# 480 bytes left unused above the right-hand tiles of SBUF

## The chip, the cores and the metric

The kernel runs on one core of one Trainium2 chip. The metric is the device time of one execution in microseconds (us), the median of several runs; lower is better.

## What is computed

All arrays are float32.

```python
def phi(x):                                   # q, k: (4, 8, 576, 64)
    proj = einsum('bhsd,df->bhsf', x, w_phi)  # 128 features
    proj = proj - max(abs(proj), axis=-1)
    return concatenate([exp(proj), exp(-proj)], axis=-1)
...
num = einsum('bhsf,bhfd->bhsd', q_p, einsum('bhsf,bhsd->bhfd', k_p, v))
den = einsum('bhsf,bhf->bhs', q_p, sum(k_p, axis=2)) + 1e-06
x = (num / den) as 2304 tokens x 512
...
h = x @ w_in                                  # 512 x 2048
x = (h * sigmoid(1.702 * h)) @ w_out          # 2048 x 512
...
p = domain_probs / (domain_probs.sum(-1) + 1e-09)
for e in range(4):
    out += p[:, e:e + 1] * (maximum(x @ w1[e], 0.0) @ w2[e])   # 512 x 1024, 1024 x 512
```

## The kernel before

The first stage is the attention: 16 pairs of heads, whose steps stand in one long written list (`ORDER`) that fixes the order on every engine. Its tiles lie in the pool `ap`. Two expert layers follow: layer 1 (sigmoid) and layer 2 (four experts with relu). They are cut into 48 units. Units 0 to 7 are layer 1 on the tokens 0 to 1279 (group 0), 8 to 15 layer 1 on the other 1024 tokens (group 1), 16 to 31 layer 2 on group 0, 32 to 47 layer 2 on group 1. A unit covers 256 hidden columns.

In a unit u the first products (x @ w_in) of u alternate with the second products (hidden @ w_out) of the unit before it, u - 1:

- Units 0 to 7 (`plain_unit`) make their first products directly: line 718 multiplies 128x512 tiles, line 741 the rest of group 0 in 128x256 tiles.
- All other units (`strassen_unit`) make seven products of six matmuls each (line 660); units of group 0 add the rest at line 741.
- The second products are line 776 in layer 1 and line 778 in layer 2. Their tile of hidden values is called `g`, or `gr` for the rest.

Each product of two float32 tiles is made of three matmuls of type fp32r: high part by high part, high by low, low by high (`PASSES`). A matmul has a stationary operand, which a weight load (PEld in the profile) puts into the array, and a moving operand, which streams through it in 512 columns (2048 bytes of each partition) or 256 columns. TensorE's order is the order of the code. Work that prepares the next units (`background`: casts and subtractions of weights on ScalarE and GpSimd, tiles of x on VectorE) is strung between the steps and pinned to them on each engine.

Two pools hold the operands, and they grow towards each other:

- `ep`, on the left (line 112), holds `xo0` to `xo6` (x, built by `build_x`), the raw weights, and `win` of the even units. The program's own allocation puts its first tile at byte 38,400 of a partition, a multiple of 512, and all of its sizes are multiples of 2048 bytes, so each of its tiles begins at a multiple of 512.
- `lp`, on the right (line 615, opened where `ap` was closed), holds `win` of the odd units (line 209: `pools[u % 2]`), `wout` of all units (line 233), `g` and `gr` (line 626), the rest `xr` of x (line 288), and the scratch tiles `sg`, `m1`, `uu` and `h`. It hangs from the right end of the usable bytes, 229,344, which is 32 more than a multiple of 64, and 480 more than a multiple of 512. All of its tiles have sizes that are multiples of 2048 bytes, so each begins 32 bytes past a multiple of 64.

The offsets of the operands inside their tiles are multiples of 512 bytes. So before the change the operands are placed like this, where "0" means at a multiple of 64 bytes and "32" means 32 bytes past one:

| line | product | stationary | moving |
|---|---|---|---|
| 718, 660, even unit | first | `win` in `ep`: 0 | `xo` in `ep`: 0 |
| 718, 660, odd unit | first | `win` in `lp`: 32 | `xo` in `ep`: 0 |
| 741, even unit | first, rest | `win` in `ep`: 0 | `xr` in `lp`: 32 |
| 741, odd unit | first, rest | `win` in `lp`: 32 | `xr` in `lp`: 32 |
| 776 | second, layer 1 | `wout` in `lp`: 32 | `g`, `gr` in `lp`: 32 |
| 778 | second, layer 2 | `g`, `gr` in `lp`: 32 | `wout` in `lp`: 32 |

The tiles of the attention's pool `ap` hang from the same end; most begin 32 bytes past a multiple of 64, a few small ones at one (of the two buffers of `kv`, one each).

Of the kernel before, what the change touches and what calls it, by code (L numbers as in the profile page):

```python
# [9 lines left out]
F32 = mybir.dt.float32  # L10
# [8 lines left out]
P = 128  # L19
# [21 lines left out]
D1 = D + 1  # L41
NB32 = 2 * S // 32
WARM = 7
ES_DVE = "0000000000000001"
FH_DVE = "0101010111011100"
BUFS = {
# [57 lines left out]
def fused(ctx: ExitStack, tc: tile.TileContext, qT, kT, v, w_phi, wg1, wg2, probs, out):  # L104
# [5 lines left out]
    dram = ctx.enter_context(tc.tile_pool(name="dram", bufs=1, space=bass.MemoryType.DRAM))  # L110

    ep = ctx.enter_context(tc.tile_pool(name="ep", bufs=1, reuse_waits="tile"))
    ap_cm = tc.tile_pool(name="ap", bufs=1, side="right", reuse_waits="tile")
    ap = ap_cm.__enter__()

# [13 lines left out]
    def warm(n):  # L129
        for _ in range(n):  # L130
            nc.tensor.matmul(ps_n[:, 0:HALF], zero[:, 0, 0, 0:P], zero[:, 0, 0, :], start=True, stop=True)

    warm(WARM)

# [212 lines left out]
    class Pair:  # L347
# [79 lines left out]
        def es(self):  # L427
            t = self.eq[:, 0, :]
            eng = nc.vector if ES_DVE[self.i] == "1" else nc.gpsimd
            eng.tensor_tensor(out=t, in0=t, in1=self.mb, op=ALU.subtract)  # L430
# [512 lines left out]
```

## Time and profile before

| | |
|---|---|
| median of 3 runs | 1320.72 us (1319.97 to 1321.62) |
| span of the profiled execution | 1319.6 us; its own time isn't listed apart from the three runs |
| attention | 0 to 161 us of the span |
| layer 1, units 0 to 15 | 161 to 549 us |
| layer 2, units 16 to 47 | 549 to 1316 us |
| TensorE busy | 1296.2 us (98%) |
| VectorE, ScalarE, GpSimd busy | 758.1 (57%), 524.6 (40%), 659.9 us (50%) |

A matmul's record runs until its last column has left the array, and the next matmul begins long before that. So the pace of TensorE isn't read from the length of a record but from the starts: the start of one group of matmuls taken from the start of the next one, divided by the number of matmuls in between. The timeline merges neighbouring matmuls of the same line and the same tiles into one row and gives its start to 0.01 us.

### The profile page before, as it was taken

What the parts mean: (1) busy time and instruction counts of PE and PEld (TensorE: products, weight loads), DVE (VectorE), ACT (ScalarE), POOL (GpSimd) and SP (SyncE); (2) the same over time, 40 slices, a digit from 0 to 9 for tenths busy, and PEclk for the clock granted to TensorE, in tenths of its full rate; (3) what the DMA queues carried; (4) which work ended last, traced back from release to release, by engine and by line L of the source; (5) the groups of instructions that cost most, each with busy time, mean ns of one, the idle gap of its engine ahead of it and who ended that gap; (6) DMA issues with size and microseconds to landing.
All of it is one profiled execution on the core that took longest, in us unless ns stands there. A gap on an engine that the chain in (4) does not pass through costs nothing.

```text
span 1319.6 us, 19956 instructions
## 1 busy us (share of the span) xinstructions
PE 1296.2 (98%) x8241; PEld 1071.5 (81%) x8241; DVE 758.1 (57%) x1084; ACT 524.6 (40%) x791; POOL 659.9 (50%) x455
## 2 busy tenths in 40 slices
PE   8998999999999999899999999999999999999998
PEld 6886888888878888788888888888888888888887
DVE  7898576776383545845444554454574545544554
ACT  5987675554355344522322232223233233232320
POOL 3677264454587776863343344334454453544530
PEclk9999999999999999899999999999999999999999
DMA  6775433333000111010011001000122110111101
GB/s 205 222 236 158 136 110 114 112 116 124 33 32 32 65 49 47 33 64 32 33 65 33 32 32 65 32 33 33 65 84 76 49 64 33 65 34 62 65 1 64
DMA packets 45709, 96.89 MB, mean 73 GB/s; under 512 B 22706, under 2 KB 22834, under 8 KB 43570
## 3 DMA queue, kind: packets, MB, share of 16 engines
q1 hardware_dynamic: 45618, 95.61, 21.8%
q8 instruction: 65, 1.06, 0.3%
q14 instruction: 26, 0.21, 0.1%
HBM read 82.42 MB, written 13.18 MB: 72 GB/s over the span
## 4 chain that ended last, share of the span: by engine, by line
PE 89%; DVE 4%; POOL 2%; ACT 2%; issue 1%; DMA 1%; SPq 0%; ACTq 0%; DVEq 0%; POOLq 0%
PE acc L778 30%; PE acc L776 13%; PE b L660 12%; PE c L660 8%; PE a L660 8%; PE a L718 3%; PE c L741 2%; PE ps_n L510 2%; PE a L741 2%; PE at L492 2%; PE b L718 1%; PE c L718 1%; PE at L445 1%; PE at L381 1%; DVE xo L136 1%
## 5 line engine op out<-in xcount | busy, mean ns | idle before, releaser
L778 PE MATMUL acc<-wout,g 128*128 128x512 f32 x1524 | 381.0, 392 | 0.0
L778 PEld LDWEIGHTS acc<-wout,g 128*128 128x128 f32 x1524 | 284.2, 188 | 62.4
L136 POOL TENSOR_TENSOR wout<-raw,wout 128x1024 fp32r<-128x1024 f32 (+1 forms) x55 | 121.5, 2214 | 399.0 <-ACT wout L234 399.0
L798 DVE SCALAR_TENSOR_TENSOR xa<-acc,pn,xa 128x512 f32<-128x512 f32 x196 | 146.7, 749 | 136.2 <-PE acc L778 136.0
L776 PE MATMUL acc<-g,wout 128*128 128x512 f32 x768 | 194.5, 395 | 2.2 <-DVE xa L790 2.2
L660 PE MATMUL b<-xo,win 128*128 128x512 f32 x720 | 186.8, 395 | 0.0
L776 PEld LDWEIGHTS acc<-g,wout 128*128 128x128 f32 x768 | 143.9, 190 | 34.0 <-DVE xa L790 2.6
L660 PEld LDWEIGHTS b<-xo,win 128*128 128x128 f32 x720 | 135.7, 189 | 31.4
L136 POOL TENSOR_TENSOR g<-sg,g 128x512 fp32r<-128x512 f32 x64 | 88.4, 1383 | 124.7 <-ACT g L635 124.7
L660 PE MATMUL c<-xo,win 128*128 128x512 f32 x480 | 125.4, 397 | 3.7 <-DVE h L667 3.7
L660 PE MATMUL a<-xo,win 128*128 128x512 f32 x480 | 124.8, 395 | 0.0
L136 POOL TENSOR_TENSOR win<-raw,win 128x1024 fp32r<-128x1024 f32 (+1 forms) x55 | 118.2, 2154 | 1.6 <-ACT win L217 1.6
L660 PEld LDWEIGHTS c<-xo,win 128*128 128x128 f32 x480 | 90.8, 189 | 25.1 <-DVE h L667 4.1
L660 PEld LDWEIGHTS a<-xo,win 128*128 128x128 f32 x480 | 90.4, 189 | 20.7
L136 POOL TENSOR_TENSOR win<-ss,win 128x1024 fp32r<-128x1024 f32 x40 | 97.0, 2426 | 10.8 <-ACT win L217 10.8
L667 DVE TENSOR_TENSOR uu<-b,m 128x512 f32<-128x512 f32 x80 | 55.3, 691 | 77.1 <-PE b L660 77.0
L639 ACT ACTIVATE g<-b 128x512 fp32r<-128x512 f32 x32 | 19.1, 598 | 192.2 <-DVE b L667 192.2
L790 DVE TENSOR_TENSOR xa<-acc,xa 128x512 f32<-128x512 f32 x84 | 57.7, 687 | 43.3 <-PE acc L776 42.8
L203 POOL TENSOR_TENSOR ss<-raw 128x256 f32<-128x256 f32 x80 | 62.1, 776 | 6.6 <-DMA raw<-in_wg_dram 5.0
L639 ACT ACTIVATE g<-a 128x512 fp32r<-128x512 f32 x32 | 19.1, 598 | 113.4 <-PE a L660 113.4
L635 ACT CAST g<-sg 128x512 fp32r<-128x512 f32 x64 | 39.7, 620 | 45.0 <-DVE sg L633 34.9
L430 POOL TENSOR_TENSOR eq<-eq,mb 128x1152 f32<-128x1152 f32 x15 | 39.8, 2652 | 34.4 <-DMA mb<-mx_d 23.0
(133 smaller groups left out, 1900.8 us busy)
## 6 DMA issues: line engine op xcount, KB each, us to landing
raw<-in_wg_dram SPq DMA_DIRECT2D x32, 1024.0 KB
raw<-in_wg_dram SPq DMA_DIRECT2D x32, 512.0 KB
mb<-mx_d SPq DMA_DIRECT2D x16, 576.0 KB
w_d<-raw SPq DMA_DIRECT2D x8, 1024.0 KB
raw<-w_d SPq DMA_DIRECT2D x8, 1024.0 KB
qraw<-in_qT_dram SPq DMA_DIRECT2D x16, 288.0 KB
kraw<-in_kT_dram SPq DMA_DIRECT2D x16, 288.0 KB
out_dram<-xa SPq DMA_DIRECT2D x18, 256.0 KB
```

The lines of the kernel that those rows point to most:

```text
L136: eng.tensor_tensor(out=dst, in0=src, in1=hi.bitcast(F32), op=ALU.subtract)
L203: nc.gpsimd.tensor_tensor(out=ss[:, n], in0=x0, in1=x1, op=op)
L430: eng.tensor_tensor(out=t, in0=t, in1=self.mb, op=ALU.subtract)
L635: nc.scalar.copy(hi, sg)
L660: nc.tensor.matmul(ps, win[self.u][:, a, w, kc * P:(kc + 1) * P], xo[i][:, e, kc, :], start=start and k_ == 0, stop=stop and k_ == 5, skip ...
L667: nc.vector.tensor_tensor(out=out, in0=ps, in1=other, op=ALU.add)
L718: nc.tensor.matmul(self.ps, win[self.u][:, a, 2 * i + kc // 2, (kc % 2) * P:(kc % 2 + 1) * P], x[:, e, kc % 2, :], start=(n == 0), stop=(n ...
L741: nc.tensor.matmul(ps, win[self.u][:, a, 2 * i + kc // 2, (kc % 2) * P:(kc % 2 + 1) * P], xo["rest"][e][:, kc, :], start=(k_ == 0), stop=( ...
L776: nc.tensor.matmul(p, w[:, a, i, t_ * P:(t_ + 1) * P], v_, **f)
L778: nc.tensor.matmul(p, v_[:, t_ * P:(t_ + 1) * P], w[:, a, i, :], **f)
L790: nc.vector.tensor_tensor(out=o, in0=ps, in1=o, op=ALU.add)
L798: nc.vector.scalar_tensor_tensor(out=o, in0=ps, scalar=col, in1=o, op0=ALU.mult, op1=ALU.add)
```

## The change

A pool `edge` is opened on the right before `ap`. It holds one tile of 120 float32 words, 480 bytes of each partition, which no instruction reads or writes. It stays open until the end, so that `ap`, and `lp` after it, hang from byte 228,864 (a multiple of 512) in place of 229,344. Every tile on the right lies 480 bytes lower; those on the left stay. No instruction, wait or transfer is added, removed or moved. `ap`, the deeper of the two pools, then ends at byte 150,016, above the last byte of `ep` at 148,992.

```diff
 WARM = 7
+EDGE = 120
...
     ep = ctx.enter_context(tc.tile_pool(name="ep", bufs=1, reuse_waits="tile"))
+    edge = ctx.enter_context(tc.tile_pool(name="edge", bufs=1, side="right"))
+    edge.tile([P, EDGE], F32, name="edge")
     ap_cm = tc.tile_pool(name="ap", bufs=1, side="right", reuse_waits="tile")
     ap = ap_cm.__enter__()
```

## Rows read from the trace of the kernel before

**Rows 1.** The page's part 4, the chain that ended last, by engine.
```profile
PE 89%; DVE 4%; POOL 2%; ACT 2%; issue 1%; DMA 1%; SPq 0%; ACTq 0%; DVEq 0%; POOLq 0%
```

**Rows 2.** Windows: stretch, length, each engine's busy us (count), clock, DMA share, GB/s.
```profile
0.00:161.00 161.00, 147.83 (x2911) 120.91 (x2912) 130.65 (x219) 122.05 (x181) 88.67 (x60) 0.98 0.65 196
...
552.00:1317.00 765.00, 763.72 (x3497) 630.13 (x3496) 389.31 (x553) 207.46 (x299) 324.43 (x223) 1.00 0.14 48
```

**Rows 3.** Timeline, TensorE, the last second products: start, length, engine, line, operands, count.
```profile
1304.65 6.99 PE L778 MATMUL acc<-wout,g 128*128 128x512 f32 x30
1311.47 1.52 PE L778 MATMUL a<-wout,g 128*128 128x512 f32 x6
...
1314.19 1.52 PE L778 MATMUL acc<-wout,g 128*128 128x512 f32 x6
```

**Rows 4.** Timeline, TensorE, layer 2: two rows of even unit 34, two of odd 35.
```profile
1016.90 1.54 PE L660 MATMUL b<-xo,win 128*128 128x512 f32 x6
1018.28 1.54 PE L778 MATMUL acc<-wout,g 128*128 128x512 f32 x6
...
1037.60 1.56 PE L660 MATMUL b<-xo,win 128*128 128x512 f32 x6
1039.00 1.55 PE L778 MATMUL acc<-wout,g 128*128 128x512 f32 x6
```

**Rows 5.** Timeline, TensorE, layer 1: four rows of even unit 2, five of odd 3.
```profile
217.73 1.58 PE L741 MATMUL c<-xr,win 128*128 128x256 f32 x12
219.15 1.57 PE L776 MATMUL acc<-g,wout 128*128 128x512 f32 x6
220.55 2.89 PE L718 MATMUL a<-xo,win 128*128 128x512 f32 x12
223.29 1.55 PE L776 MATMUL acc<-g,wout 128*128 128x512 f32 x6
...
231.64 2.97 PE L718 MATMUL a<-xo,win 128*128 128x512 f32 x12
234.44 2.92 PE L776 MATMUL acc<-g,wout 128*128 128x512 f32 x12
...
245.62 1.60 PE L741 MATMUL c<-xr,win 128*128 128x256 f32 x12
247.06 1.55 PE L776 MATMUL acc<-g,wout 128*128 128x512 f32 x6
248.45 2.97 PE L718 MATMUL a<-xo,win 128*128 128x512 f32 x12
```

**Rows 6.** Windows, one whole unit each: units 2, 3, 30, 31, 34 and 35.
```profile
203.87:231.64 27.77, 27.77 (x146) 23.74 (x144) 18.56 (x28) 15.29 (x28) 13.20 (x10) 1.00 0.33 114
231.64:259.65 28.01, 28.01 (x145) 23.77 (x144) 20.79 (x29) 14.96 (x28) 13.46 (x10) 1.00 0.33 113
917.16:943.45 26.29, 26.29 (x127) 21.99 (x126) 12.16 (x18) 6.63 (x10) 10.01 (x7) 1.00 0.11 41
943.45:969.90 26.45, 26.45 (x127) 22.01 (x126) 22.37 (x25) 11.30 (x15) 12.20 (x4) 1.00 0.12 41
1014.14:1034.80 20.66, 20.66 (x91) 16.89 (x90) 9.79 (x15) 5.85 (x8) 10.04 (x7) 1.00 0.13 51
1034.80:1055.64 20.84, 20.84 (x91) 16.90 (x90) 9.82 (x15) 5.84 (x8) 10.06 (x7) 1.00 0.15 51
```

**Rows 7.** Timeline, TensorE, where it waits in units 8 and 15 (idle before in brackets).
```profile
388.81 2.72 PE L776 MATMUL acc<-g,wout 128*128 128x512 f32 x6 [2.17 <-DVE xa L790]
...
547.30 2.93 PE L660 MATMUL c<-xo,win 128*128 128x512 f32 x6 [3.72 <-DVE h L667]
550.03 1.48 PE L660 MATMUL a<-xo,win 128*128 128x512 f32 x3
```

**Rows 8.** Groups by shape, VectorE, whole span: busy us, mean ns, idle before.
```profile
L790 DVE TENSOR_TENSOR xa<-acc,xa 128x512 f32<-128x512 f32 x84 | 57.7, 687 | 43.3 <-PE acc L776 42.8
L667 DVE TENSOR_TENSOR uu<-b,m 128x512 f32<-128x512 f32 x80 | 55.3, 691 | 77.1 <-PE b L660 77.0
```

## The prediction

> **What bounds the kernel.** I read the chain that ended last first: TensorE holds 89% of it [rows 1]. Then the windows by stage: in the attention, up to 161 us, VectorE and ScalarE are nearly as full as TensorE, but from 552 us to the end TensorE is busy for 763.72 of 765 us while VectorE is busy for half of it [rows 2]. So in the expert layers a nanosecond on each matmul is a nanosecond on the end, and the change can matter only through TensorE's pace there, at which the timeline's starts are to be read.
>
> **The settled pace.** At the kernel's end, groups of second products stand back to back: from 1311.47 to 1314.19 us twelve matmuls start, 226.7 ns each; the thirty before them take 6.82 us, 227.3 ns each [rows 3]. Twelve 256-column matmuls of line 741 in odd unit 3 take 1.44 us, 120.0 ns each [rows 5]. The 106.7 ns between the two is 256 columns at 2.4 GHz, so each matmul carries 13.3 ns that don't depend on its columns. I call 226.7 and 120.0 ns settled.
>
> **Where the pace is worse.** Three kinds of rows are slower, and they sort by how operands lie against 64 bytes.
> First, stationary at 32 and moving at 0 (first products of odd units): six matmuls of line 660 take 1.40 us in unit 35, 233 ns each [rows 4]; twelve of line 718 take 2.80 us in unit 3, also 233 ns [rows 5]. The same products in even units, both operands at 0, take 1.38 us for six [rows 4] and 2.74 us for twelve, 228 ns [rows 5].
> Second, any change between a group with moving operands at 0 and one at 32: the even unit's 1.38 us for six is 230 ns though both of its operands are at 0, because it stands between groups of line 778 [rows 4]; in rows 3, with no such change, the pace is settled. A change of line alone costs nothing: in unit 3 the twelve of line 741 follow 256-column ones of line 776, all at 32, and are settled [rows 5].
> Third, going from 256 to 512 columns: the six of line 776 behind line 741 in unit 3 take 1.39 us, 0.03 over six settled ones [rows 5].
> The surplus of the first kind is 233.3 - 226.7 = 6.7 ns, which is the time of eight columns at 1.2 GHz, and eight float32 words are 32 bytes. I read this as the two streams, stationary and moving, being in step or out of step within 64 bytes. It is an inference: in this trace "0" also means the left tiles and "32" the right ones. A 256-column group with moving at 32 and stationary at 0 is even a little quicker than settled: 1.42 us for twelve, 118.3 ns each, in unit 2 [rows 5].
>
> **The change, part by part.**
> The unused tile has no instruction, so it costs no time itself. Everything in the table of operands becomes 0 and 0. The first two kinds of surplus then have no cause; the third stays.
>
> Per unit, with the settled paces and the counts in the code (each window counts one or two neighbours too):
> - Units 1 to 7 have 96 matmuls of 512 columns and 48 of 256: 96 x 0.2267 + 48 x 0.1200 = 27.52 us. Unit 2 lasts 27.77, unit 3 28.01 [rows 6]. Three changes from 256 to 512 columns in each keep 0.09. Saved: even 0.16, odd 0.40. Three even and four odd: 2.1 us.
> - Units of group 1 have 90 of 512: 20.40 us. Unit 34 lasts 20.66, unit 35 20.84 [rows 6]. Saved: 0.26 and 0.44. Ten even (10 to 14, 34 to 46) and twelve odd (9 to 15, 33 to 47): 7.9 us.
> - Units 17 to 31 have 102 of 512 and 24 of 256: 26.00 us. Unit 30 lasts 26.29, unit 31 26.45 [rows 6]. Two changes of width keep 0.06. Saved: 0.23 and 0.39. Seven even, eight odd: 4.7 us.
> - Units 0, 8, 16 and 32 are even and mixed: some 0.2 each, 0.8 us. An estimate from the even ones above.
> Together 15.5 us.
>
> What hides or takes back: in two places TensorE waits for VectorE, 2.17 us in unit 8 and 3.72 us in unit 15, where VectorE builds x for the next group and the adds stand behind that in its queue [rows 7]. What TensorE gains in these two units (0.2 and 0.44) lengthens the waits: minus 0.6 us. Elsewhere the next to be late is VectorE, busy for about half of each unit [rows 6], so nothing else takes the gain back. Net 14.9 us.
>
> Other engines read and write moved tiles as well. VectorE's add with two operands in right-hand tiles takes 691 ns, the same add on `xa`, which lies at 0, takes 687 [rows 8]: 0.6% at most, off the path in the expert layers. In the attention, where VectorE is busy for 130.65 us [rows 2], 0.6% either way is 0.8 us. How attention's float32 matmuls and its loads take the move isn't shown; I bound all that by twice this, 1.5 us either way, and take nothing, because ops that differ only so hardly differ in rows 8.
>
> Against the span of 1319.6 us this gives 1304.7. The runs' median stands 1.1 us above that span; with it, 1305.8 us.
>
> The Trainium skill speaks against the change at this point. The page "TensorE: Matmul & The Clock Gate", Part 2, says that TensorE has two independent SBUF read ports, and that loading the next tile's weights doesn't steal read bandwidth from the running matmul. By that rule the place of the one operand against the other is of no account and the time stays at 1320.7; the trace disagrees in the first kind of row, 233 against 228 ns for the same product. The page "SBUF — State Buffer", Specifications, gives 16-byte cachelines; 32 bytes past a multiple of 64 begins such a line too, so by that as well nothing changes.
>
> **The rivals.**
> *Nothing changes: it is left against right, not the offset.* If the slower pairs are slow because one operand lies in the low part of SBUF and the other in the high part, 480 bytes do nothing: 1320.7 us, within 0.7. For it: in this trace every 0 among the expert operands is a left tile and every 32 a right one. Against it: a surplus of 32 bytes' worth of columns, and that a mere change of width, with no change of place, disturbs the next six matmuls by about as much as a change of place does.
> *Only the steady surplus goes.* The odd units become like the even ones, while the disturbance at each change between lines 660 and 778 stays, because it comes from changing tiles. Then the odd units save 0.18 x 12 + 0.16 x 8 + 0.24 x 4 = 4.4 us [rows 6]: 1316.3 us. Against it stands the change from line 776 to line 741, which disturbs nothing.
> *Slower: the clock falls once more.* Behind the 3.72 us wait six matmuls take 2.73 us, 455 ns each, which is the 1.2 GHz level [rows 7]; each six at that level costs 1.37 us. If VectorE's queue at another change of layer becomes the bound, as it would if its operations on moved tiles got slower, and TensorE idles there in the same way, two to three such groups cost 2.7 to 4.1 us. It decides only where the pace gains under 0.1 us a unit, that is together with the first rival: 1324 us. Nothing in rows 8 speaks for such slower operations.
>
> **How the numbers follow.** Full effect 0.74, range of its own 1302 to 1309: down by the attention's 1.5 and by a wait in units 8 or 15 that shortens, up by 1.5 and by some of the disturbance staying. Steady surplus only, 0.11. Nothing, 0.11. Slower, 0.04. The prediction is the first: 1305.8. The range goes from 1302 to 1316.6 and so takes in the second; the third and fourth, 0.15, are left out. A measurement of this kernel tells some 0.2%, 2.6 us, from no change. Faster by more than that: 0.74 + 0.11 = 0.85; same: 0.11; slower: 0.04.
>
> **What would show it.** In the changed kernel's timeline every six of lines 660 and 778 (three lines further down there) should start 1.36 us after the one before, in odd and even units alike; units 34 and 35 should both last 20.40 us, unit 31 26.06. If odd and even become alike at 20.66, the second rival holds; at 20.66 and 20.84 as now, the first. Line 741 of even units should go from 118.3 to 120.0 ns. The waits in units 8 and 15 should be there still and a little longer. The prediction is wrong if the settled pace itself moves, or if the attention no longer ends near 161 us.

## The result and the profile after

The changed kernel takes 1307.42 us (median of 6 runs, 1305.51 to 1311.85), the kernel before, measured beside it, 1321.19 us (median of 6 runs, 1319.97 to 1328.59). The ratio is 0.9886, 95% interval 0.9865 to 0.9906: 1.1% faster. 1305.8 us was forecast, with a range of 1302 to 1316.6. The profiled execution took 1306.83 us, its span 1305.1 us; 1304.7 was forecast for the span.

From here the lines of the changed kernel stand three further down: 660 is 663, 718 is 721, 741 is 744, 776 is 779 and 778 is 781.

The changed kernel's timeline of TensorE, columns as in rows 3: the start of even unit 34, and the last group and the start of the next unit, odd 35.

```profile
1004.47 1.52 PE L663 MATMUL a<-xo,win 128*128 128x512 f32 x6
1005.83 1.52 PE L781 MATMUL acc<-wout,g 128*128 128x512 f32 x6
1007.19 1.52 PE L663 MATMUL b<-xo,win 128*128 128x512 f32 x6
1008.55 1.52 PE L781 MATMUL acc<-wout,g 128*128 128x512 f32 x6
...
1023.51 1.52 PE L663 MATMUL c<-xo,win 128*128 128x512 f32 x6
1024.87 1.52 PE L663 MATMUL a<-xo,win 128*128 128x512 f32 x6
1026.23 1.52 PE L781 MATMUL acc<-wout,g 128*128 128x512 f32 x6
```

Every group of six starts 1.36 us after the one before it, 226.7 ns for each matmul, in the even unit and in the odd one, across changes of line and of tiles. In rows 4 it was 1.38 us in the even and 1.40 us in the odd unit.

The windows of whole units of the changed kernel, columns as in rows 2: units 2, 3, 30, 31, 34 and 35, which answer to rows 6.

```profile
206.01:233.59 27.58, 27.58 (x145) 23.77 (x144) 18.58 (x28) 15.11 (x27) 13.20 (x10) 1.00 0.34 115
233.59:261.17 27.58, 27.58 (x145) 23.77 (x144) 20.69 (x29) 14.84 (x27) 13.41 (x10) 1.00 0.34 115
908.80:934.84 26.04, 26.04 (x127) 22.02 (x126) 12.16 (x18) 6.63 (x10) 9.99 (x7) 1.00 0.13 41
934.84:960.88 26.04, 26.04 (x127) 21.89 (x126) 22.29 (x25) 11.23 (x15) 12.16 (x4) 1.00 0.12 41
1004.47:1024.87 20.40, 20.40 (x91) 16.90 (x90) 9.75 (x15) 5.84 (x8) 10.03 (x7) 1.00 0.16 51
1024.87:1045.27 20.40, 20.40 (x91) 16.90 (x90) 9.76 (x15) 5.84 (x8) 10.03 (x7) 1.00 0.16 52
```

Odd and even are alike: 27.58, 26.04 and 20.40 us, where 27.61, 26.06 and 20.40 had been worked out.

The timeline of the changed kernel in layer 1 (unit 2), which answers to rows 5, and the two waits of rows 7.

```profile
219.78 1.60 PE L744 MATMUL c<-xr,win 128*128 128x256 f32 x12
221.22 1.55 PE L779 MATMUL acc<-g,wout 128*128 128x512 f32 x6
222.61 2.88 PE L721 MATMUL a<-xo,win 128*128 128x512 f32 x12
225.33 1.52 PE L779 MATMUL acc<-g,wout 128*128 128x512 f32 x6
...
389.30 1.66 PE L779 MATMUL acc<-g,wout 128*128 128x512 f32 x6 [2.48 <-DVE xa L793]
390.79 1.52 PE L663 MATMUL b<-xo,win 128*128 128x512 f32 x6
...
543.99 1.86 PE L663 MATMUL c<-xo,win 128*128 128x512 f32 x6 [3.91 <-DVE h L670]
545.65 1.48 PE L663 MATMUL a<-xo,win 128*128 128x512 f32 x3
```

Twelve of line 721 take 2.72 us, settled. The six behind the 256-column ones still take 1.39 us: the price of the change of width has stayed. Twelve of line 744 take 1.44 us in this even unit, where they took 1.42. The waits for VectorE are 2.48 and 3.91 us, 0.31 and 0.19 longer than before.

The start of the first product of the expert layers, line 718 before and 721 after: the kernel before, then the changed one.

```profile
161.24 2.09 PE L718 MATMUL a<-xo,win 128*128 128x512 f32 x8
...
```
```profile
163.69 1.64 PE L721 MATMUL a<-xo,win 128*128 128x512 f32 x6
...
```

The attention took 2.45 us more in this profile. From there to the end of the last matmul the expert layers took 1154.5 us before and 1137.4 after: 17.1 us less. The longer attention takes 2.45 of it back, so 14.6 are left.

### The profile page after: what moved, and what is told of

It is laid out like the page before. It is cut to its first block, busy times and chain, and to the rows that moved or that the text cites. A ratio compares the mean times of both kernels' runs of the same rounds, so it can differ in the third digit from the quotient of the medians.

```text
span 1305.1 us, 19956 instructions
## 1 busy us (share of the span) xinstructions
PE 1278.4 (98%) x8241; PEld 1069.6 (82%) x8241; DVE 757.4 (58%) x1084; ACT 523.8 (40%) x791; POOL 659.6 (51%) x455
## 4 chain that ended last, share of the span: by engine, by line
PE 86%; DVE 5%; POOL 3%; ACT 2%; DMA 2%; issue 2%; SPq 0%; POOLq 0%; ACTq 0%; DVEq 0%
PE acc L781 30%; PE acc L779 12%; PE b L663 12%; PE c L663 8%; PE a L663 8%; PE a L721 3%; PE c L744 2%; PE a L744 2%; PE ps_n L513 2%; PE b L721 1%; PE at L495 1%; PE c L721 1%; POOL eq L433 1%; PE at L448 1%; DMA qraw<-in_qT_dram 1%
## 5 line engine op out<-in xcount | busy, mean ns | idle before, releaser
L781 PE MATMUL acc<-wout,g 128*128 128x512 f32 x1524 | 376.8, 389 | 0.0
L663 PE MATMUL b<-xo,win 128*128 128x512 f32 x720 | 182.7, 389 | 0.0
L663 PE MATMUL c<-xo,win 128*128 128x512 f32 x480 | 122.1, 390 | 3.9 <-DVE h L670 3.9
```

Of the source, the lines that this page charges most:

```text
L663: nc.tensor.matmul(ps, win[self.u][:, a, w, kc * P:(kc + 1) * P], xo[i][:, e, kc, :], start=start and k_ == 0, stop=stop and k_ == 5, skip ...
L781: nc.tensor.matmul(p, v_[:, t_ * P:(t_ + 1) * P], w[:, a, i, :], **f)
```

## Experiments

Two questions were open: whether the longer attention is the price of moving `ap`, and whether the offset within 64 bytes is what counts. The second matters because the change puts all operands at the same place not only within 64 bytes, but within 512, so its result can't tell these apart.

**Only `lp` moved.** The unused tile is opened where `ap` has been closed.

```diff
+    edge = ctx.enter_context(tc.tile_pool(name="edge", bufs=1, side="right"))
+    edge.tile([P, EDGE], F32, name="edge")
     lp = ctx.enter_context(tc.tile_pool(name="lp", bufs=1, side="right", reuse_waits="tile"))
```

> The 480 bytes are left out only once the attention is over: its pool ap stays at its old place, lp moves as in the changed kernel. The attention of the changed kernel ended 2.4 us later than before (163.7 against 161.2 us of the span). Theory 'the move of ap makes the attention longer': here the attention ends near 161.2 us again and the expert units last as in the changed kernel (20.40 us each in group 1), so some 1304 to 1305 us. Theory 'the attention scatters from run to run, whatever its addresses': its end lies anywhere from 161 to 165 us in a profile, and the median is as that of the changed kernel, 1306 to 1308 us.

1308.45 us, ratio to the kernel before 0.9892 (95% interval 0.986 to 0.9923). The expert units are those of the changed kernel. The attention, with `ap` at its old addresses, ended later than in any other profile and later than either theory had it (timeline, first expert product):

```profile
167.22 0.95 PE L721 MATMUL a<-xo,win 128*128 128x512 f32 x3
```

**Only `ap` moved.** The unused tile's pool is closed again right behind `ap`, so that `lp` lies where it lay before.

```diff
     ap_cm.__exit__(None, None, None)
+    edge_cm.__exit__(None, None, None)
```

> The 480 bytes are left out only during the attention: ap moves, lp lies where it lay before. Expert units as before the change (20.66 and 20.84 us in group 1, 26.30 and 26.45 in layer 2 of group 0). Theory 'the move of ap makes the attention longer': its end near 163.7 us, 1323 us in all. Theory 'scatter': 1320 to 1322 us like the kernel before.

1321.89 us, ratio 0.9996 (0.9976 to 1.0016): no change. The units are those of the kernel before, 20.66 and 20.84 us, and the attention ended at 162.56 us. So the gain belongs to `lp` alone.

**Both kernels once more**, unchanged, for a second profile of each.

> The kernel before once more, for a second profile of its attention. Theory 'the attention scatters by itself': its end falls somewhere else between 160 and 168 us, the units last as in the first profile (20.66 and 20.84 us in group 1). Theory 'the addresses of ap set it': 161.2 us again.

> The changed kernel once more, for a second profile of its attention. Theory 'the attention scatters by itself': its end falls somewhere else between 160 and 168 us, the units last 20.40 us as in the first. Theory 'the addresses of ap set it': 163.7 us again.

The first expert product, in the kernel before and in the changed one:

```profile
164.35 1.87 PE L718 MATMUL a<-xo,win 128*128 128x512 f32 x7
```
```profile
159.28 0.93 PE L721 MATMUL a<-xo,win 128*128 128x512 f32 x3
```

These executions took 1323.97 and 1302.56 us. The order is turned round: 161.24 and 163.69 us in the first profiles, 164.35 and 159.28 in the second ones. Their units last 20.66 and 20.84 us, and 20.40 us, as in the first ones. The move of `ap` isn't what made the attention longer; it scatters by some microseconds from run to run. Over all profiles of this document, it ended between 161.24 and 167.22 us with `ap` at its old place (five profiles), and between 159.28 and 164.36 us with `ap` moved (eight). At the two extremes the waits for the transfer of the row maxima (`mb`) differ as well. From the waits of the first 168 us (engine and line, who is waited for, us in total, times, longest), the changed kernel's second profile first, then the run with only `lp` moved (the same line of code stands at 433 and at 431):

```profile
POOL eq L433 <- DMA mb<-mx_d: 17.7, 7, 6.5
```
```profile
POOL eq L431 <- DMA mb<-mx_d: 33.6, 10, 7.1
```

GpSimd waited 17.7 us for it where the attention ended first, 33.6 where it ended last. In between the two don't always go together: with 33.0 us of these waits the attention ended at 161.30 us (the run with `win` moved by 16 and 32 bytes, below), with 19.3 us at 164.24 (all operands at 32 modulo 64, below). What makes the attention scatter stays open.

**All operands at 32 modulo 64.** The right side stays, and 32 bytes are left unused on the left.

```diff
+LEFT = 8
...
+    left = ctx.enter_context(tc.tile_pool(name="left", bufs=1))
+    left.tile([P, LEFT], F32, name="left")
     ep = ctx.enter_context(tc.tile_pool(name="ep", bufs=1, reuse_waits="tile"))
```

> The right side lies as before the change; on the left 32 bytes are left unused ahead of ep, so that all operands of the expert layers begin 32 bytes past a multiple of 64. Theory 'stationary and moving operands have to lie at the same offset within 64 bytes, whichever it is': all units settled as in the changed kernel, 20.40 us in group 1 and 26.04 in layer 2 of group 0, some 1304 us with the attention as before. Theory 'an operand has to begin at a multiple of 64 bytes': no better than before the change, 20.66 us and more, 1320 us or above.

**32 unused bytes on the right in place of 480.**

```diff
-EDGE = 120
+EDGE = 8
```

> The unused tile has 32 bytes in place of 480: the right side lies at multiples of 64 bytes, but 64 past a multiple of 128 and 448 past one of 512, while the left lies at multiples of 512. Theory 'the offset within 64 bytes counts': units as in the changed kernel, 20.40 us, 1305 to 1308 us. Theory 'a larger unit counts (128 or 512 bytes)': odd units of group 1 stay slower than even ones, 1316 to 1321 us.

1317.97 us, ratio 0.996 (0.9938 to 0.9983), and 1319.11 us, ratio 0.9971 (0.9953 to 0.999). The first of the two went against its first theory (the units aren't settled) and, in the time, against its second (1320 us or above); the second run came out as the theory of a larger unit had it. The starts of units 34, 35 and 36 in the run with all operands at 32 modulo 64, then in the run with 32 bytes on the right:

```profile
1010.51 1.53 PE L663 MATMUL a<-xo,win 128*128 128x512 f32 x6
...
1031.19 1.54 PE L663 MATMUL a<-xo,win 128*128 128x512 f32 x6
...
1051.98 1.31 PE L663 MATMUL a<-xo,win 128*128 128x512 f32 x5
```
```profile
1009.89 1.53 PE L663 MATMUL a<-xo,win 128*128 128x512 f32 x6
...
1030.57 1.54 PE L663 MATMUL a<-xo,win 128*128 128x512 f32 x6
...
1051.36 1.31 PE L663 MATMUL a<-xo,win 128*128 128x512 f32 x5
```

Both give 20.68 and 20.79 us for units 34 and 35, so neither is settled, though all operands have the same offset within 64 bytes in both, and all are at multiples of 64 in the second. The two runs share one thing: from the left tiles to the right ones the distance is 448 bytes modulo 512, that is 192 modulo 256. So distance counts and not place, and the unit in which it counts is larger than 64 bytes.

**How far apart, one operand at a time.** On top of the changed kernel, `win` alone is moved inside a tile that is 512 bytes larger: by 16 bytes in even and 32 in odd units, then 64 and 448, then 128 and 256.

```diff
-        t = pools[u % 2].tile([P, 2, 8, 256], F32R, tag="win%d" % (u % 2), name="win", bufs=1)
+        x = (4, 8)[u % 2]
+        t = pools[u % 2].tile([P, 4224], F32R, tag="win%d" % (u % 2), name="win", bufs=1)
+        t = t[:, x:x + 4096].rearrange("p (a w f) -> p a w f", a=2, w=8)
```

> On top of the changed kernel, where all operands lie at multiples of 512 bytes, only the stationary operand of the first products is moved: win begins 16 bytes further in even units and 32 further in odd ones; everything else, the moving operands above all, stays at multiples of 512. A unit of group 1 that is settled lasts 20.40 us; with 42 first products, a surplus of s ns on each makes it 20.40 + 0.042 s. Theory 'the time goes by the size of the offset': odd units 20.68 us as for the 32 bytes of the kernel before (6.7 ns each), even ones half of that, 20.54. Theory 'any offset other than a multiple of 512 disturbs alike': even and odd about the same, 20.6 to 20.7. Theory 'the sign counts, stationary ahead or behind': before the change win lay 32 bytes behind (480 modulo 512), here it is ahead, and the odd units are not at 20.68.

> As the run with 16 and 32 bytes, but win begins 64 bytes past a multiple of 512 in even units and 448 past one (64 behind the next) in odd ones. Theory 'offset within 64 bytes': both settled, 20.40 us in group 1. Theory 'offset within 512 bytes', from the runs with 32 unused bytes on the right: the odd units have some 4.4 ns on each of 42 products, 20.40 + 0.18 = 20.58 us; even units the same if only the distance counts, and another time, perhaps below 20.40, if the sign counts: there 256-column products with the moving operand 64 bytes behind the stationary one ran 3.7 ns quicker than settled.

> As the run with 16 and 32 bytes, but win begins 128 bytes past a multiple of 512 in even units and 256 past one in odd ones. Theory 'offset within 128 bytes': both at 20.40 us in group 1. Theory 'within 256': even units disturbed (20.5 to 20.7), odd ones at 20.40. Theory 'within 512': both disturbed.

These are single runs: 1310.64, 1313.75 and 1316.02 us. Such a time holds the attention's scatter as well, so the units are compared, as the traces give them. The starts of units 34, 35 and 36, in the same order of runs (line 663 stands at 665 here):

```profile
1005.71 1.56 PE L665 MATMUL a<-xo,win 128*128 128x512 f32 x6
...
1026.16 1.56 PE L665 MATMUL a<-xo,win 128*128 128x512 f32 x6
...
1046.88 1.33 PE L665 MATMUL a<-xo,win 128*128 128x512 f32 x5
```
```profile
1007.35 1.56 PE L665 MATMUL a<-xo,win 128*128 128x512 f32 x6
...
1028.19 1.55 PE L665 MATMUL a<-xo,win 128*128 128x512 f32 x6
...
1048.71 1.33 PE L665 MATMUL a<-xo,win 128*128 128x512 f32 x5
```
```profile
1011.38 1.56 PE L665 MATMUL a<-xo,win 128*128 128x512 f32 x6
...
1032.09 1.53 PE L665 MATMUL a<-xo,win 128*128 128x512 f32 x6
...
1052.50 1.33 PE L665 MATMUL a<-xo,win 128*128 128x512 f32 x5
```

As lengths of a unit, where 20.40 us is settled:

| `win` past a multiple of 512 by | unit | over settled |
|---|---|---|
| 0 | 20.40 us | 0 |
| 16 bytes | 20.45 | 0.05 |
| 32 | 20.72 | 0.32 |
| 64 | 20.84 | 0.44 |
| 128 | 20.71 | 0.31 |
| 256 | 20.41 | 0.01 |
| 448 (64 before the next) | 20.52 | 0.12 |

The surplus isn't proportional to the distance, and it isn't the same ahead and behind (64 and 448; the one was measured in even units, the other in odd ones, which are alike where all is settled). At 256 it is gone but for 0.01 us, at 128 it is not: of the distances tried, only 0 and 256 leave the units settled. "Modulo 256" below stands for that; not every distance in between was tried. The surplus here includes that of the second products, whose own operands are all at multiples of 512 and which follow disturbed groups.

**The same on the other side of the comparison: 224 bytes.** First the unused tile on the right has 224 bytes in place of 480 (`EDGE = 56`), so that right and left differ by 256.

> The unused tile has 224 bytes in place of 480: the right side lies 256 bytes past a multiple of 512, the left at multiples of 512. Theory 'offset within 256 bytes or less': all units as in the changed kernel, 20.40 us in group 1, 26.04 in layer 2 of group 0. Theory 'offset within 512 bytes': disturbed at the odd units and at each change between left and right, 20.5 to 20.8 us.

Then the right side stays as it was before the change, and 224 bytes are left unused on the left (`LEFT = 56`, ahead of `ep`, as above), so that every operand of the expert layers begins 32 bytes past a multiple of 64 and 224 past one of 256.

> The right side lies as before the change; on the left 224 bytes are left unused ahead of ep. All operands of the expert layers then begin 224 bytes past a multiple of 256, that is 32 past a multiple of 64 and none at one. Theory 'all operands need the same offset within 256 bytes, whichever': settled, 20.40 us for every unit of group 1, 26.04 in layer 2 of group 0, and 1304 to 1309 us with the attention's scatter. Theory 'operands have to begin at a multiple of 64 bytes': 20.66 us and more, 1320 us or above.

The starts of units 34, 35 and 36, first with 224 bytes on the right, then on the left:

```profile
1003.12 1.52 PE L663 MATMUL a<-xo,win 128*128 128x512 f32 x6
...
1023.52 1.52 PE L663 MATMUL a<-xo,win 128*128 128x512 f32 x6
...
1043.92 1.30 PE L663 MATMUL a<-xo,win 128*128 128x512 f32 x5
```
```profile
1008.47 1.52 PE L663 MATMUL a<-xo,win 128*128 128x512 f32 x6
...
1028.87 1.52 PE L663 MATMUL a<-xo,win 128*128 128x512 f32 x6
...
1049.27 1.29 PE L663 MATMUL a<-xo,win 128*128 128x512 f32 x5
```

20.40 us for every one. The first took 1305.48 us in a single run, the second 1309.61 us, ratio 0.9885 (0.9852 to 0.9919). So, in the second of them, the whole gain comes without moving anything on the right, and without one operand at a multiple of 64 bytes. Neither is shown to beat the changed kernel: they differ from it by less than the attention scatters.

## Why the prediction was right, and where it was not

**Bound and pace: right.** TensorE's pace set the end in the expert layers, and the gain came out as time on the end, but for what the waits in units 8 and 15 kept. The settled pace of 226.7 ns, read from twelve matmuls at the end of the kernel before [rows 3], is the pace of nearly all 512-column matmuls of the changed kernel.

**The sum, term by term:**

| term | forecast | measured |
|---|---|---|
| units 1 to 7 | 2.1 us | 2.2 |
| group 1, without units 8, 15, 32 | 7.5 | 7.5 |
| units 17 to 31 | 4.7 | 5.0 |
| units 0, 16 and 32 | 0.6 | 0.2 |
| units 8 and 15, net of the waits | 0.0 | 2.1 |
| attention | 0 (within 1.5) | -2.45 |
| span | 14.9 | 14.5 |

The measured terms are differences of unit lengths in the two first profiles; they add up to 14.6, and the spans, given to a tenth, differ by 14.5. The rows in which only the pace counts, the first four, come to 14.9 us forecast and 14.9 measured. The medians differ by 13.8 us, and in the runs with only `lp` moved and with 224 bytes on the left, whose paces are the same, by 14.8 and 14.3.

**Two terms were off and offset each other, by luck.** The bound on the attention, 1.5 us either way, was too narrow: it was taken from VectorE's 0.6% in rows 8, while the attention's end scatters between 159.28 and 167.22 us over the profiles, which one profile can't show. An attention that no longer ends near 161 us was named as a sign of being wrong; with this scatter it couldn't serve as one.

In units 8 and 15 the gain was to be lost to the waits for VectorE. The waits did grow, but in these two profiles TensorE's clock differs behind them. The windows of units 8, 15 and 16, before and then after, columns as in rows 2:

```profile
371.20:398.80 27.60, 25.43 (x116) 20.84 (x115) 21.57 (x23) 12.46 (x17) 22.58 (x12) 0.94 0.10 38
523.30:548.75 25.45, 21.73 (x91) 17.29 (x90) 21.24 (x20) 13.18 (x17) 22.62 (x12) 0.95 0.12 42
548.75:574.30 25.55, 25.55 (x116) 21.18 (x115) 16.31 (x21) 11.23 (x17) 17.99 (x14) 0.92 0.13 42
```
```profile
371.50:397.60 26.10, 23.61 (x116) 19.69 (x115) 21.68 (x23) 12.46 (x17) 22.82 (x12) 1.00 0.12 40
520.00:544.80 24.80, 20.89 (x91) 16.73 (x90) 20.56 (x20) 13.15 (x17) 22.33 (x12) 1.00 0.13 43
544.80:570.30 25.50, 25.26 (x116) 20.85 (x115) 17.47 (x21) 10.99 (x17) 18.33 (x15) 0.93 0.13 42
```

In unit 8 the granted clock is 0.94 of 2.4 GHz before and 1.00 after, and the unit is 1.5 us shorter. That isn't an effect of the pace: unit 8 lasts 26.1 us in both profiles of the changed kernel, but 27.5 in the run with only `lp` moved and in the run with 224 bytes on the left, whose paces are the same; and it lasts 27.6 us in both profiles of the kernel before, but 26.0 in the run with only `ap` moved, whose paces are those of the kernel before. Where the clock did the same, then, the gain in unit 8 is lost to the wait, as forecast. Unit 15 is 0.65 us shorter in the first profiles, and no shorter in the second ones: 25.48 us before, 25.44 after. The wait in unit 8 isn't certain either: in three runs above (all operands at 32 modulo 64, `win` moved by 16 and 32, and by 64 and 448 bytes) TensorE doesn't wait there, and the unit lasts 23.7 to 24.1 us. Why wasn't followed up.

**Smaller readings.** The median was put 1.1 us above the span; all runs whose span is on record stand 1.7 to 1.9 us above it. VectorE was said to be busy for about half of each unit; in rows 6 it is so in units 30, 34 and 35, but at 67 to 85% in units 2, 3 and 31. No new wait came of it.

**The reason given for the pace: wrong in its size.** The step that failed is the reading of 6.7 ns as eight columns, hence 32 bytes, hence "in step or out of step within 64 bytes". The rate of 1.2 GHz doesn't fit the rows themselves: rows 6 show a granted clock of 1.00, that is 2.4 GHz, in these units, at which 6.7 ns is the time of sixteen columns, or 64 bytes. The runs show a distance modulo 256 bytes, and a surplus that doesn't go by the bytes. The table of operands was right all the same, because 480 bytes bring right and left to the same place modulo 512, and so modulo 256. Had the change left out 32 bytes, the same argument would have given 1305.8 us, and the run with 32 bytes took 1319.11. The rows of before could not tell this, since they hold one distance only; the prediction said that "0" and "32" were also left and right, but not that 32 was also 224 modulo 256.

**The rivals.** That nothing changes (left against right) is excluded: left and right are as far apart as ever, 512-column products with one operand on each side are settled. That the disturbance between the groups stays is excluded by the 1.36 us at each change of line. In the expert layers the clock fell nowhere anew: in the changed kernel it is 1.00 in every unit shown above but 16, where it had fallen before as well.

The Trainium skill's page "TensorE: Matmul & The Clock Gate", Part 2, has it that loading the next weights takes no read bandwidth from the running matmul. What the prediction drew from this rule, that the place of the one operand against the other is of no account, doesn't hold here: moving only the stationary operand by 64 bytes made a unit 0.44 us longer. Whether that time is lost in reading, no run shows.

**What stays open** is the mechanism. The traces hold one hint: in unit 35 a matmul of line 660 is 396 ns long in the kernel before and 389 in the changed kernel, while a weight load takes 188 ns in both; but a matmul's end is modelled by the profiler. That the two streams of TensorE meet in something that repeats every 256 bytes of a partition fits all runs, but no run shows it; nor why a disturbed group hands its delay on to the next.

## What to carry to other kernels

Where matmuls follow each other without a gap, compare the pace (starts, not lengths) of groups that do the same work with tiles from different pools: a difference that goes by the buffer's parity can be one of address. On this chip, with fp32r operands, the cure was to bring all stationary and moving operands to the same place modulo 256 bytes, and 224 unused bytes on either side sufficed. When a change fits more than one unit, forecast with the unit left open, and test it with an amount at which the units disagree.

## What the runs showed of the hardware

A settled stream of fp32r matmuls, at a granted clock of 1.00, starts one every 226.7 ns with 512 columns and 120.0 ns with 256, so 13.3 ns of each don't depend on the columns. The distances tried between stationary and moving operand other than 0 and 256 bytes added up to some 7 ns to a 512-column matmul (6.7 ns in unit 35 of the kernel before). With 256 columns it can go the other way: 118.3 ns in unit 2 before the change, 120.0 after. A change from 256 to 512 columns costs 0.03 us over the next six. Beginning at a multiple of 64 bytes is neither needed (224 unused bytes on the left: 20.40 us a unit) nor enough (32 on the right: 20.68 and 20.79 us).
